# A recurrent-memory attention kernel with a gated feed-forward: Wo pieces multiplied in pairs, the late half of Wo moved behind two Wq pieces, a Wk eviction moved ahead, and the turning of x spread over the first step

## The chip, the cores and the metric

The kernel runs on one core of one Trainium2 chip. The metric is the time of one execution on the device in microseconds (us), as a median over runs; lower is better. The core's engines are TensorE (in the profile PE for matmuls and PEld for weight loads), VectorE (DVE), ScalarE (ACT), GpSimd (POOL) and SyncE (SP). SP, ACT and POOL issue DMAs; each has its own DMA queue. Each engine runs its own instructions strictly in the order in which the program lists them, and waits on semaphores for the others.

## The reference

Two branches over the same x of 2048 rows by 1024 (bfloat16) are mixed by a gate per row. Branch A is a transformer with a recurrent memory; branch B is a feed-forward.

```python
def _A_ref(x, mem0, Wq, Wk, Wv, Wo, seg_len):      # 32 heads of 128, M = 8, seg_len = 32
    ...
    for s in range(n_seg):                          # 64 segments
        xs = x[:, s * seg_len:(s + 1) * seg_len, :].copy()
        h = jnp.concatenate([mem, xs], axis=1)      # 8 + 32 = 40 rows
        q = jnp.einsum('btd,dhe->bhte', h, Wq)
        k = jnp.einsum('btd,dhe->bhte', h, Wk)
        v = jnp.einsum('btd,dhe->bhte', h, Wv)
        scores = jnp.einsum('bhqe,bhke->bhqk', q, k) * scale
        scores = jnp.where(mask[None, None], scores, -1000000000.0)
        p = _softmax(scores, axis=-1)
        o = jnp.einsum('bhqk,bhke->bhqe', p, v)
        o = jnp.einsum('bhte,hed->btd', o, Wo)
        mem = o[:, :M, :].copy()
        outs.append(o[:, M:, :])
    return jnp.concatenate(outs, axis=1)

def _B_ref(x, w_gate, w_up, w_down):
    return _gelu(x @ w_gate) * (x @ w_up) @ w_down

g = _sigmoid((x * gate_w).sum(-1, keepdims=True))
return g * a + (1 - g) * b
```

Each segment needs the memory rows that the segment before it produced, so the 64 segments form a chain.

## The kernel before

**Stages.** First the 16 tiles of x (128 rows each) are turned so that the model dimension lies on the partitions (`do_x`, L440). Then 64 steps run, one per segment. At the end the outputs of the rows that feed no memory are projected (L902 to L919), and the feed-forward follows (L951 on).

**Rows of a step.** The 40 rows of a segment are split. The 8 memory rows and 24 rows of x, 32 together, go through the step (`hT`). The remaining 8 rows of x are gathered from four segments at a time into a group of 32 rows (`hR`). Their projections are called fills: `fill` (L740) multiplies, `fill_evac` (L764) evicts, `fill_put` (L775) turns and writes to DRAM (`qk_scr`, `v_scr`). A step does one fill or two (`FILL`, L791; two in the steps after segments 0 and 1 of each four); `load_qk` (L476) and `load_v` (L481) fetch a segment's part back with POOL DMAs, `load_r` (L472) fetches the next group's rows. Where no second fill is to be done, `warm` (L754) multiplies for nothing.

**Weights.** Wq, Wk, Wv and Wo are each cut into 16 pieces of 512 KB: two halves of 16 heads (index u) by eight pieces i. All 64 do not fit into SBUF. Some places are held by a fixed piece; 14 are shared by the pieces (m, 0, i) and (m, 1, i) (`PAIRS`, L297: two each of Wk and Wq, four of Wv, six of Wo). A step works on one half first (r = 0) and on the other after it (r = 1), and the next step starts with the half that is there. So a shared place is loaded once per step, as soon as the piece of r = 0 has been multiplied (`spent`, L389); that is 14 loads of 512 KB per step, issued by SP. The copies of the shared Wo pieces in `wo_scr` are written in steps 1 to 12 (`keep`, L364) and read from then on.

**Order.** `HEAD` and `BODY` (L309, L310) list blocks of four pieces; `walk` (L315) makes of them the order of all pieces on TensorE:

```python
HEAD = [("k", 0, 0), ("o", 1, 1), ("q", 0, 0), ("v", 0, 0), ("k", 0, 1), ("q", 0, 1), ("v", 0, 1)]
BODY = [(m, r, h) for m, r in (("k", 1), ("q", 1), ("o", 0), ("v", 1)) for h in range(2)] + [("o", 1, 0)]
```

The block `("o", 1, 1)`, the late half of the second Wo half, belongs to the step before and runs after the first four Wk pieces of the new step. `seq` (L304) gives the order of the eight pieces of a half. `plan` (L807) hangs all other work on places of this walk: `on("q", 1, 2, f)` runs f just before piece 2 of Wq, r = 1. The place in the walk fixes an operation's place in the order of its engine, not only on TensorE: an operation of ACT, POOL or SP stands behind all operations of that engine that were hung on earlier places.

**One projection piece** (`proj`, L688): for q, k and v four matmuls of 512 columns (L699), one for each group of 32 partitions of the PSUM bank. A Wo piece (L711) is eight matmuls of 256 columns, into the half b = i // 4 of the columns of bank `XO`, with the heads j = i % 4.

**Attention of a half.** `evac` (L601) copies the projection from PSUM to a staging tile with ACT; `trans` turns it (four transposes, L611) and copies it with DVE (L597) into `kT` or `qT`. `put_rest` (POOL, L787) adds the eight rest columns to `kT`. `scores` (L624) multiplies (L627, L633) and runs the softmax down to `tAB`, the turned probabilities (L639 to L652). `attend` (L654) multiplies with `vA` (L661, L666), which ACT evicted from the Wv bank, and `take` copies the result to `oT`. `rest_o` (POOL) keeps the rest rows in `oRc`, from where SP writes them to DRAM (L872).

**Shared memory.** Staging tiles have no place of their own (L289): `stage["k"]` lies on `kT`, and so does `pAB`; `stage["q"]` lies on `qT`, and so does `tAB`; `stage["o"]` lies on `oT`, and so does `vA`. `oRc` (512 bytes per partition) and `a_bf` (512 bytes) follow each other. A writer waits until all readers of what lies there are done; for a DMA that reads, until it has landed.

**Memory chain.** When a half of the columns of Wo is complete, `fold` (L719) adds the two halves of the partitions with two DVE operations (L722, L723) into `a_bf`. `next_mem` (L726) turns the memory rows (two transposes, L732) and copies them (L735) into the next step's `hT`: half 0 before the first Wk piece, half 1 before piece 4. Piece i of Wk, Wq and Wv reads only chunk i of `hT`. `a_bf` is written to DRAM (`a_scr`) by a POOL DMA (L889).

**First step.** Before step 0, all 16 calls of `do_x` run: eight transposes into a PSUM bank, three copies (ACT and DVE), DMAs of the turned tile to DRAM (ACT's queue), the gate's product on POOL (L463, into one buffer `gp`) and its sum on DVE (L465). Eight buffers `px` hold x; a load of tile T + 8 waits for the product of tile T. The work buffers of this stage lie on the places of Wo. Then step 0 does seven fills itself (`fill0`, L802).

## Time and profile before

| | |
|---|---|
| median of 3 runs | 2394.21 us (2392.74 to 2399.93) |
| the profiled execution's own time | 2389.05 us |
| its span, first to last instruction | 2387.2 us |
| mean granted TensorE clock | 0.973 |
| busy share of the span: PE / PEld / DVE / ACT / POOL | 89% / 47% / 44% / 22% / 18% |
| DMA | 639.69 MB, mean 268 GB/s |
| scores of the first half in steps 0, 1 and 63 start at | 100.0, 142.4 and 1721.4 us |
| first feed-forward matmul starts at | 1799.2 us |

So the 64 steps take most of the span, about 25 us each after the first ones; the feed-forward takes the last 588 us. How to read the lines below: "busy" is the time in which an engine worked on the group; "idle before" is the time that the engine stood still just ahead of it, with what ended the wait. In the timeline each row is a start, a duration, the engine, the line of the kernel, the operation and what it writes and reads; x32 means that 32 like instructions were merged into one row. The chain of waits is the sequence of work that ended last, each link released by the one before. A matmul of a stream is shown with its whole latency, so of a row of n matmuls the pace is to be read and not the single duration.

### The profile page before, as it was taken

To read this page: it belongs to the slowest core of one execution; us is meant where nothing else is said; L and a number is where in the kernel's file an instruction comes from. 1 tells how busy PE (TensorE), PEld (TensorE's weight loads), DVE (VectorE), ACT (ScalarE), POOL (GpSimd) and SP (SyncE) were. 2 spreads that over 40 slices of the span, in tenths; PEclk is the share of its full clock that TensorE was granted. 3 is DMA by queue.
4 is the path that set the end of the run, shared out by engine and by line. 5 is a ranking of instruction groups with operands and counts; after the bars stand their busy time and mean duration, and the time that the engine had idled before them with its cause. 6 is when DMAs were issued, how large, how long until landed. Compare 5 with 4: busy or idle time off the path is not lost.

```text
span 2387.2 us, 78943 instructions
## 1 busy us (share of the span) xinstructions
PE 2135.7 (89%) x35875; PEld 1119.7 (47%) x35900; DVE 1050.7 (44%) x2438; ACT 515.9 (22%) x985; POOL 431.0 (18%) x821
## 2 busy tenths in 40 slices
PE   2588888898898999898998999988889999999999
PEld 1244444454454545444544555554454444444444
DVE  3244444444444444444444444454414436264363
ACT  1121212222222222222222222221203213032130
POOL 5222222222222222222222222221100000000000
PEclk6699999999999999999999999999999999999999
DMA  9889989998998989899898999998976160622530
GB/s 359 331 292 301 325 305 325 347 319 310 321 314 309 328 305 327 309 316 327 299 315 307 324 333 331 317 327 315 332 247 212 63 219 18 234 66 89 180 103 18
DMA packets 261469, 639.69 MB, mean 268 GB/s; under 512 B 28264, under 2 KB 102760, under 8 KB 261136
## 3 DMA queue, kind: packets, MB, share of 16 engines
q1 hardware_dynamic: 237312, 597.66, 71.6%
q0 software_dynamic: 13888, 26.31, 3.7%
q10 hardware_dynamic: 9936, 10.69, 1.3%
q8 instruction: 282, 4.62, 0.8%
q14 instruction: 51, 0.42, 0.1%
HBM read 596.85 MB, written 37.68 MB: 266 GB/s over the span
## 4 chain that ended last, share of the span: by engine, by line
PE 65%; DVE 14%; DMA 9%; issue 6%; ACT 5%; POOL 1%; ACTq 0%; POOLq 0%; SPq 0%
PE pb L699 16%; PE pb L960 14%; PE pb L711 9%; PE pb L1014 5%; PE pb L611 5%; PE pb L748 4%; DMA sl<-in_A_Wo_dram 3%; DVE tAB L652 3%; PE pb L911 2%; ACT kS L594 2%; PE pb L995 2%; PE pb L633 2%; DMA sl<-wo_scr 2%; PE pb L758 2%; DVE pb L640 2%
## 5 line engine op out<-in xcount | busy, mean ns | idle before, releaser
L699 PE MATMUL pb<-sl,hT 128*32 128x512 bf16 x12288 | 766.1, 382 | 7.7 <-issue 6.8
L699 PEld LDWEIGHTS pb<-sl,hT 128*32 128x32 bf16 x12288 | 350.3, 97 | 260.7 <-issue 16.6
L711 PE MATMUL pb<-sl,oT 128*32 128x256 bf16 x8192 | 307.3, 277 | 49.1 <-issue 29.7
L711 PEld LDWEIGHTS pb<-sl,oT 128*32 128x32 bf16 x8192 | 196.3, 97 | 121.1 <-issue 40.4
L748 PE MATMUL pb<-sl,hR 128*32 128x512 bf16 x3072 | 233.1, 397 | 15.2 <-issue 14.0
L960 PE MATMUL pb<-xT,wg 128*128 128x512 bf16 x896 | 211.7, 379 | 0.7
L960 PE MATMUL pb<-xT,wu 128*128 128x512 bf16 x896 | 211.6, 379 | 0.0
L594 ACT ACTIVATE kS<-pb 128x512 bf16<-128x512 f32 x190 | 113.4, 597 | 453.9 <-PE pb L699 359.8
L682 POOL COPY oRc<-oT 128x128 bf16<-128x128 bf16 x128 | 96.6, 754 | 345.2 <-DVE oT L597 342.7
L722 DVE COPY part<-pb 64x256 f32<-64x256 f32 x128 | 54.0, 422 | 229.0 <-PE pb L711 225.6
L597 DVE CAST oT<-pb 128x160 bf16<-128x160 f32 x382 | 105.6, 318 | 110.4 <-PE pb L666 110.4
L641 ACT ACTIVATE E<-pb 128x320 bf16<-128x320 f32 x128 | 55.9, 437 | 439.6 <-DVE pb L640 439.6
L1014 PE MATMUL pb<-wd,GT 128*128 128x512 bf16 x657 | 145.1, 379 | 2.7 <-DMA wd<-in_B_w_down_dram 1.9
L960 PEld LDWEIGHTS pb<-xT,wg 128*128 128x128 bf16 x896 | 87.2, 98 | 108.0 <-DVE GT L976 3.7
L597 DVE COPY kT<-pb 128x512 bf16<-128x512 bf16 x128 | 54.3, 424 | 188.4 <-PE pb L611 180.7
L960 PEld LDWEIGHTS pb<-xT,wu 128*128 128x128 bf16 x896 | 87.6, 98 | 105.7
L968 ACT ACTIVATE s<-pb 128x512 f32<-128x512 f32 x112 | 66.8, 596 | 312.3 <-PE pb L960 312.3
L969 DVE SCALAR_TENSOR_TENSOR tp<-s,pb 128x512 f32<-128x512 f32 x112 | 77.0, 687 | 124.7 <-ACT s L968 124.5
L639 DVE TENSOR_REDUCE st<-pb 128x8 f32<-128x320 f32 x128 | 63.0, 492 | 140.6 <-PE pb L633 140.6
L787 POOL COPY kT<-qkr 128x128 bf16<-128x128 bf16 x128 | 37.6, 294 | 460.0 <-DVE kT L597 368.8
L748 PEld LDWEIGHTS pb<-sl,hR 128*32 128x32 bf16 x3072 | 86.7, 99 | 70.9 <-issue 31.5
L973 DVE SCALAR_TENSOR_TENSOR tp<-tp,pb 128x512 f32<-128x512 f32 x112 | 77.0, 687 | 78.7 <-ACT tp L972 78.7
(84 smaller groups left out, 2096.7 us busy)
## 6 DMA issues: line engine op xcount, KB each, us to landing
sl<-wo_scr SPq DMA_DIRECT2D x342, 512.0 KB, 7.0
sl<-in_A_Wv_dram SPq DMA_DIRECT2D x268, 512.0 KB, 10.4
sl<-in_A_Wk_dram SPq DMA_DIRECT2D x142, 512.0 KB, 5.5
sl<-in_A_Wq_dram SPq DMA_DIRECT2D x142, 512.0 KB, 7.5
wd<-in_B_w_down_dram SPq DMA_DIRECT2D x42, 1024.0 KB, 5.6
sl<-in_A_Wo_dram SPq DMA_DIRECT2D x52, 512.0 KB, 7.7
wdF<-in_B_w_down_dram SPq DMA_DIRECT2D x7, 1024.0 KB, 7.8
wo_scr<-sl SPq DMA_DIRECT2D x12, 512.0 KB, 11.5
```

Of the source, the lines that this page charges most:

```text
L594: op("act", lambda e: e.activation(o, i, ACTF.Copy), rd=rd, wr=wr)
L597: op("dve", lambda e: e.tensor_copy(o, i), rd=rd, wr=wr)
L611: ins = e.transpose(PBV[TT][:, j * 128:(j + 1) * 128], st[:, j * 128:(j + 1) * 128], ident[:, :])
L652: op("dve", lambda e: e.transpose(tAB[:, :], pAB[:, 0:512]), rd=[pAB.r()], wr=[tAB.r()], after=[fin])
L682: op("pool", lambda e: e.tensor_copy(oRc[:, :, 16 * u:16 * u + 16].rearrange("p c x -> p x c"), oT[:, :, :, 32:40].rearrange("p g j c -> p ...
L699: ins = e.matmul(PB[bk][32 * g:32 * g + 32, :], lhsT=h[:, i, :], rhs=w[:, g * 512:(g + 1) * 512], start=(n == 0), stop=(n == 7))
L711: ins = e.matmul(PB[XO][32 * g:32 * g + 32, 256 * b:256 * b + 256], lhsT=oT[:, j, x, 0:32], rhs=w[:, c:c + 256], start=(r == 0 and n == 0 ...
L748: ins = e.matmul(PB[b][32 * g:32 * g + 32, :], lhsT=h[:, k[2], :], rhs=w[:, g * 512:(g + 1) * 512], start=(n == 0), stop=(n == 7))
L960: ins = e.matmul(PB[bk][:, 0:FB], lhsT=w[:, kc, cc:cc + 128], rhs=xT[:, :, :, kc, :].rearrange("p t i c -> p (t i) c"), start=(kc == 0), s ...
L969: op("dve", lambda e, hg=hg, t=t: e.scalar_tensor_tensor(out=t[:, :], in0=s1[:, :], scalar=1.0, in1=hg, op0=ALU.add, op1=ALU.mult), rd=[BK ...
L973: op("dve", lambda e, hu=hu, t=t: e.scalar_tensor_tensor(out=t[:, :], in0=t[:, :], scalar=1.0, in1=hu, op0=ALU.add, op1=ALU.mult), rd=[BK( ...
L1014: ins = e.matmul(PB[bank[2 * k + hf]][:, :], lhsT=GT[:, j, tb * 128:(tb + 1) * 128], rhs=w[:, jj, hf * 512:(hf + 1) * 512], start=(j == 0) ...
```

## The change

Four things are changed in the steps, and the start.

1. For r = 0, Wo pieces i and i + 4 (the same heads, the two halves of the columns) are multiplied together: eight matmuls of 512 columns in place of sixteen of 256. The places of Wo become one tensor `wall`, so that one operand can reach into two of them; the order is 0, 4, 1, 5, 2, 6, 3, 7, and both places are given back after the pair.
2. The late half of Wo (r = 1, pieces 4 to 7) runs after the first two Wq pieces of the next step. Its `fold`, the second fill's eviction and `load_v` move with it, from the place ahead of Wq piece 0 to that ahead of piece 2; `fill_put` goes from Wv piece 0 to 2 and `next_mem` of half 1 from Wv piece 1 to 3.
3. In steps 1 to 63 the second Wk half is evicted at Wq piece 1 (r = 1) and not at the start of Wo, into a new staging tile that lies on `oRc` and `a_bf`. The eviction into `vA` moves from Wq piece 2 to 3. The DMA that writes `a_bf` to `a_scr` moves from ("q", 1, 0) to ("k", 0, 4).
4. Four tiles of x are turned ahead of step 0 and the other twelve in it, in banks `XO` and `SS`; the gate and the loads follow them, and the fills of r = 1 in step 0 are hung on different Wq pieces.

```diff
-        stage = {n: al(n + "S", [128, 512], at=t.off) for n, t in (("k", kT), ("q", qT), ("o", oT))}
+        assert a_bf.off == oRc.off + 512
+        stage = {n: al(n + "S", [128, 512], at=t.off) for n, t in (("k", kT), ("q", qT), ("o", oT), ("p", oRc))}
...
+            if (m, r) == ("o", 0):
+                return [i + x for i in range(4) for x in (0, 4)]
...
-        HEAD = [("k", 0, 0), ("o", 1, 1), ("q", 0, 0), ("v", 0, 0), ("k", 0, 1), ("q", 0, 1), ("v", 0, 1)]
-        BODY = [(m, r, h) for m, r in (("k", 1), ("q", 1), ("o", 0), ("v", 1)) for h in range(2)] + [("o", 1, 0)]
+        HEAD = [("k", 0, 0, 4), ("q", 0, 0, 2), ("o", 1, 4, 8), ("q", 0, 2, 4), ("v", 0, 0, 4), ("k", 0, 4, 8), ("q", 0, 4, 8), ("v", 0, 4, 8)]
+        BODY = [(m, r, 0, 8) for m, r in (("k", 1), ("q", 1), ("o", 0), ("v", 1))] + [("o", 1, 0, 4)]
...
-        slots = [al(f"sl{n}", [128, 2048]) for n in range(len(hosts))]
+        nkqv = sum(h[0][0] != "o" for h in hosts)
+        slots = [al(f"sl{n}", [128, 2048]) for n in range(nkqv)]
+        wall = al("wall", [128, len(hosts) - nkqv, 2048])
+        slots += [_V(wall, n) for n in range(len(hosts) - nkqv)]
...
-            b = 6 + T % 2
+            b = (XO, SS)[T % 2]
...
-        for T in range(NT):
+        do_x(0)
+        load_h(0, "pool")
...
+        for T in range(1, min(NT, 4)):
             do_x(T)
...
+            elif r == 0:
+                j = i % 4
+                w4 = 4 * LQ
+                if n % 2 == 0:
+                    wa, wb = slots[home[k]], slots[home[k[0], k[1], i + 4]]
+                    na, nb = wa.n, wb.n
+
+                    def f(e):
+                        for hp in range(2):
+                            for g in range(4):
+                                x = 2 * hp + g // 2
+                                c = 512 * x + 256 * (g % 2)
+                                ins = e.matmul(PB[XO][32 * g:32 * g + 32, :], lhsT=oT[:, j, x, 0:32],
+                                               rhs=wall[:, na:nb + 1:nb - na, c:c + 256], start=(n == 0 and hp == 0),
+                                               stop=False, skip_group_check=True)
+                        return ins
+                    op("pe", f, rd=[oT.r(j * w4, (j + 1) * w4), wa.r(), wb.r()], wr=[BK(XO)])
+                if n % 2:
+                    spent((*k[:2], i - 4))
+                    spent(k)
+                return
...
             if s == 0:
+                on("k", 0, 0, lambda: some_x(4, 6))
                 on("k", 0, 0, lambda: fill0("k", 0, B0, "k"))
                 if NG > 1:
                     on("k", 0, 0, lambda: fill0("k", 0, B1, "o", 1, hR1))
-                on("k", 0, 0, lambda: [first(("o", u, i)) for u in range(2) for i in range(8)])
+                on("q", 0, 0, lambda: some_x(6, 8))
+                on("q", 0, 0, lambda: [load_x(NPX + n) for n in range(4, 8)])
+                on("q", 0, 0, lambda: (firsts("k", 1), firsts("q", 1)))
                 on("q", 0, 0, lambda: fill0("q", 0, B1, "q"))
+                on("v", 0, 0, lambda: some_x(8, 12))
                 on("v", 0, 0, lambda: fill0("v", 0, B2, "o"))
+                on("k", 0, 4, lambda: some_x(12, 16))
...
+                on("k", 0, 4, gate)
+                on("k", 0, 5, lambda: (firsts("v", 1), firsts("o", 0), firsts("o", 1)))
...
-            on(*(("k", 1, 1) if s == 0 else ("q", 1, 2)), lambda: evac(bank_of["v", 0], vA, "act"))
+            on(*(("k", 1, 1) if s == 0 else ("q", 1, 3)), lambda: evac(bank_of["v", 0], vA, "act"))
...
-            on("o", 0, 0, lambda: evac(bank_of["k", 1], stage["k"], "act"))
+            on(*(("q", 1, 1) if s else ("o", 0, 0)), lambda: evac(bank_of["k", 1], stage["p" if s else "k"], "act"))
             if s > 0:
                 on("o", 0, 0, lambda: attend(ua, ((0, "dve"), (1, "dve"))))
-            on("o", 0, 0, lambda: trans(kT, "k"))
+            on("o", 0, 0, lambda: trans(kT, "p" if s else "k"))
...
             if two:
-                on("q", 0, 0, lambda: fill_evac(*fl[1], B0, "o"), **nx)
-                on("v", 0, 0, lambda: fill_put(*fl[1], "o"), **nx)
-            on("q", 0, 0, lambda: fold(s, 1), **nx)
-            on("q", 0, 0, lambda: load_v(s + 1), **nx)
-            on("v", 0, 1, lambda: next_mem(s, 1), **nx)
-            on("q", 1, 0, lambda: op("pool", lambda e: e.dma_start(a_scr[s].rearrange("g r c -> (g r) c"), a_bf[:, :]), rd=[a_bf.r()],
+                on("q", 0, 2, lambda: fill_evac(*fl[1], B0, "o"), **nx)
+                on("v", 0, 2, lambda: fill_put(*fl[1], "o"), **nx)
+            on("q", 0, 2, lambda: fold(s, 1), **nx)
+            on("q", 0, 2, lambda: load_v(s + 1), **nx)
+            on("v", 0, 3, lambda: next_mem(s, 1), **nx)
+            on("k", 0, 4, lambda: op("pool", lambda e: e.dma_start(a_scr[s].rearrange("g r c -> (g r) c"), a_bf[:, :]), rd=[a_bf.r()],
                                      wr=[("D", "a", s)], lane="st"), **nx)
```

`_V` is a view of one place of `wall` with the same attributes as a tile of its own; `firsts(m, r)` issues the first load of the eight pieces of a half; `some_x(lo, hi)` calls `do_x` for those tiles; `gate` holds the three operations (L512 to L515) that turn the row sums into the gate.

66 lines of the change are left out of this document (36 added, 30 removed).

## Prediction

> **What bounds the kernel now.** I read the chain of waits first. By engine it says:
>
> ```profile
> PE 65%; DVE 14%; DMA 9%; issue 6%; ACT 5%; POOL 1%; ACTq 0%; POOLq 0%; SPq 0%
> ```
>
> TensorE sets two thirds; a third is work on which TensorE waits. The steps have to be opened one by one. I take step 35 and read the timeline by engine, from its first scores (L627 at 1022.29) to the second. TensorE:
>
> ```profile
> 1022.29 0.31 PE L627 MATMUL pb<-mS,ident 128*128 128x320 bf16 x1
> ...
> 1026.71 0.50 PE L661 MATMUL pb<-tAB,vA 32*128 32x40 bf16 x16
> 1027.04 0.20 PE L666 MATMUL pb<-tAB,vB 32*128 32x64 bf16 x4
> 1027.36 0.40 PE L611 MATMUL pb<-ident,kS 128*128 128x128 bf16 x4
> 1027.69 0.63 PE L711 MATMUL pb<-sl,oT 128*32 128x256 bf16 x16
> 1028.37 0.38 PE L611 MATMUL pb<-ident,qS 128*128 128x128 bf16 x4
> 1028.68 1.06 PE L711 MATMUL pb<-sl,oT 128*32 128x256 bf16 x32
> 1029.67 0.31 PE L627 MATMUL pb<-mS,ident 128*128 128x320 bf16 x1
> ```
>
> ACT and DVE in the same stretch:
>
> ```profile
> 1024.41 0.59 ACT L594 ACTIVATE vA<-pb 128x512 bf16<-128x512 f32 x1
> 1026.71 0.60 ACT L594 ACTIVATE kS<-pb 128x512 bf16<-128x512 f32 x1 [1.70 <-PE pb L699]
> 1027.30 0.60 ACT L594 ACTIVATE qS<-pb 128x512 bf16<-128x512 f32 x1
> ```
>
> ```profile
> 1027.30 0.56 DVE L597 CAST oT<-pb 128x160 bf16<-128x160 f32 x2 [0.69 <-PE pb L666]
> 1027.79 0.42 DVE L597 COPY kT<-pb 128x512 bf16<-128x512 bf16 x1
> 1028.14 0.55 DVE L597 CAST oT<-pb 128x160 bf16<-128x160 f32 x2
> 1028.79 0.42 DVE L597 COPY qT<-pb 128x512 bf16<-128x512 bf16 x1
> ```
>
> The attention of the first half starts at 1026.71, and the second scores at 1029.67, so 2.96 us later. In between TensorE turns K only after ACT has evicted it (1026.71 to 1027.31), and the eviction had waited for the softmax, since its staging tile lies on `pAB`. The vA eviction, done at 1025.00, is 1.7 us ahead of its use.
>
> **Part 1, paired pieces and an early Wk eviction.** First the pace of both kinds of matmul, from the chain of waits:
>
> ```profile
> 1039.37 0.86 PE pb L699 x16
> 1040.24 0.87 PE pb L711 x32
> ```
>
> 512 columns take 53.8 ns, 256 take 27.2: two merged matmuls cost what one wide one costs, so the merging gains nothing where matmuls stream at this pace. In the first Wo half they don't: there the 32 end 0.99 us after their start (1028.68 to 1029.67). The rest comes from the order. With K evicted beforehand, counted from the start A of the attention: its matmuls leave TensorE free at A+0.31; K is turned until A+0.71; the first oT copy ends at A+0.87 (1027.30 + 0.28), so pair 0 runs from A+0.93 to A+1.36 (8 x 53.8 ns); Q is turned until A+1.74, its eviction being done at A+1.19; pairs 1 and 2 end at A+2.60. On DVE the copies end about A+2.55. The scores start at A+2.62 and not A+2.96: **0.34 us less a step, 63 steps, -21 us**. Bounds: DVE, which has the same four copies, allows no more; if nothing but the eviction helped it would be 0.1 us, -6. The order 0, 4, 1, 5 lets piece 1 be fetched third and not second. It is used only after the eight Wv pieces (32 matmuls, 1.7 us), the second softmax and three more pieces, and I cost this at nothing; without that cover a load of 512 KB more ahead of it is 2.0 us at the mean 268 GB/s.
>
> **Part 2, what the early eviction waits for.** The new staging tile lies on `oRc` and `a_bf`, so the eviction must wait until the DMA that writes `a_bf` to DRAM has landed. In ACT's order vA stands behind it, and the attention waits for vA. POOL's timeline in step 35:
>
> ```profile
> 1017.95 0.55 POOL L482 DMA_DIRECT2D vB<-v_scr  x1 [3.61 <-DVE a_bf L723]
> 1018.49 0.56 POOL L473 DMA_DIRECT2D hR<-xr_scr  x1
> ...
> 1023.21 0.55 POOL L889 DMA_DIRECT2D a_scr<-a_bf  x1
> ```
>
> The DMA is moved from 1023.21 to right behind the vB load, where the hR load stands in this step. The late Wo half comes 8 matmuls later (8 x 53.8 ns = 0.43 us), so it is issued at 1018.49 + 0.43 = 1018.92. When it lands, the DMA issues of 300 to 1500 us bound (the last number is the median to landing):
>
> ```profile
> vB<-v_scr POOLq DMA_DIRECT2D x48, 64.0 KB, 6.7
> ...
> a_scr<-a_bf POOLq DMA_DIRECT2D x47, 64.0 KB, 5.8
> hR<-xr_scr POOLq DMA_DIRECT2D x12, 64.0 KB, 7.3
> ```
>
> By its own row (5.8, at its old place) it lands at 1024.7. Then come two evictions of 0.60 and 0.05 to the matmul: attention possible at 1026.0, and nothing is lost against 1026.71. By the hR row (the same size, the same place in the queue) it lands at 1026.2, the attention starts at 1027.5 and 0.8 us is lost. I take 0.7: the place behind the vB load counts for more than the direction. **63 x 0.7 = +44 us**, bounds 0 and, by a late vA below, 2.0 us (126). That a late vA stops TensorE is seen in step 33, where another DMA held it:
>
> ```profile
> 976.98 0.60 ACT L594 ACTIVATE vA<-pb 128x512 bf16<-128x512 f32 x1 [3.26 <-DMA qk_scr<-oS]
> 977.63 0.27 PE L661 MATMUL pb<-tAB,vA 32*128 32x40 bf16 x16 [2.03 <-ACT vA L594]
> ```
>
> The Trainium skill, page "DMA: Bandwidth & Descriptors", section "Anatomy of one DMA — SWDGE (gpsimd) path", gives about 2.0 us plus bytes over 436 GB/s per DMA. For 64 KB that would be, as an estimate from that page, 2.2 us, the DMA would be back 5 us before it is needed, and the sum would be 44 us lower. The trace disagrees: all three rows above are 2.6 to 3.3 times as long, with the other queue full of 512 KB loads.
>
> **Part 3, the late Wo half behind two Wq pieces.** The matmuls are the same, and their loads have 0.43 us more. What that can bring is bounded by the page's row of the Wo matmuls:
>
> ```profile
> L711 PE MATMUL pb<-sl,oT 128*32 128x256 bf16 x8192 | 307.3, 277 | 49.1 <-issue 29.7
> ```
>
> Of the 49.1 us idle ahead of them 29.7 have no releaser; 19.4 remain for all Wo matmuls and steps, so -19 at most; I take 0, since a load that is late by more than 0.43 us stays late. SP issues the two Wq loads about 1 us earlier (the 32 Wo matmuls, 0.87, no longer stand before them). The vB load on POOL goes 0.43 us later and, by its 6.7, lands at 1025.1, still ahead of the attention. What is lost is cover: after `next_mem` of half 1, three Wv pieces ran before Wk piece 4 needed its result, now one.
>
> ```profile
> 1017.74 0.23 PE L732 MATMUL pb<-ident,a_bf 64*128 64x64 bf16 x2
> ```
>
> ```profile
> 1018.00 0.17 DVE L735 COPY hT<-pb 128x32 bf16<-128x32 bf16 x1 [0.34 <-PE pb L732]
> ```
>
> The copy ends at 1018.17; with 0.05 for the semaphore and 0.1 for the weights (the first oT copy to the first Wo matmul above takes as long) Wk could start at 1018.33. One Wv piece (0.22) covers from 1017.97 to 1018.19. **0.15 us x 63 = +9 us**, bounds 0 and 0.25 (+16). The `fold` keeps its distance of five pieces; `fill_put` keeps its place one piece ahead.
>
> **Part 4, fewer instructions.** 32 matmuls and 32 weight loads a step are gone. TensorE has gaps with no releaser; its instructions come by DMA on a queue of their own (packets, MB, share of the engines' span):
>
> ```profile
> q8 instruction: 282, 4.62, 0.8%
> ```
>
> ```profile
> 1031.99 0.39 PE L748 MATMUL pb<-sl,hR 128*32 128x512 bf16 x1 [0.59 <-issue]
> ```
>
> The gaps follow the stretches of short matmuls, of which the first Wo half is one. "issue" is 6% of the chain, 143 us over the span; I take 0.1 us a step off, **-6 us**, bounds 0 and 0.25 (-16). The skill's page "Runtime: NRT & Kernel Launch", section "Instruction fetch mechanics", calls the crossing of a 16 KiB block mostly hidden. By it this term is 0 and the sum 6 us higher; the gap of 0.59 above speaks for the trace.
>
> **Part 5, the start.** POOL before and in step 0:
>
> ```profile
> 69.52 2.12 POOL L463 TENSOR_TENSOR gp<-px,gwb 128x1024 f32<-128x1024 bf16 x1 [1.93 <-DVE dl L465]
> 75.05 0.82 POOL L783 DMA_DIRECT2D qk_scr<-kS  x1 [3.42 <-DVE kS L780]
> 80.98 0.76 POOL L783 DMA_DIRECT2D qk_scr<-oS  x1 [5.11 <-DMA qk_scr<-kS]
> 87.64 0.75 POOL L783 DMA_DIRECT2D qk_scr<-qS  x1 [5.90 <-DMA qk_scr<-oS]
> 88.39 2.20 POOL L769 DMA_DIRECT2D v_scr<-oS  x4
> 94.21 0.56 POOL L478 DMA_DIRECT2D qkr<-qk_scr  x1 [3.62 <-DMA qk_scr<-qS]
> ```
>
> The first attention in step 0 follows at:
>
> ```profile
> 105.14 0.32 PE L661 MATMUL pb<-tAB,vA 32*128 32x40 bf16 x16 [4.32 <-DMA vB<-v_scr]
> ```
>
> The last product of x ends at 71.6, and only then come three writes of fills, one after another as they share a lane, before the loads that the first attention needs. In the change the fills of Wk and Wq run between the tiles, so their writes have landed long before the last product. They cost POOL their issue (3 x 0.8), the four v writes (2.2) and one wait of 5.1; the products end at 71.6 + 9.7 = 81, and the qkr load is issued there and not at 94.2: **-13 us**. Bounds: -21 if POOL lost nothing (94.2 less 73), 0 if the loads of Wo, whose places hold x until the last tile, decide step 0.
>
> **Sum.** -21 + 44 + 9 - 6 - 13 = +13 us on the profiled execution's own 2389.05 (its span is 2387.2). That execution lies 5.2 below the median of 2394.21; against the median the change gives **2407 us**, slower by 0.5%.
>
> **Rivals.**
> - *The write of a_bf is back in time* (place: ACT's eviction at Wq piece 1; it decides where the DMA lands before about 1025.4 in step 35, 6.5 us after its issue). For it: the a_scr row of 5.8, and the page's rule above, whose result this is; Wq loads that start earlier leave less in the queues. Against: the vB and hR rows. Then Part 2 is 0: 2407 - 44 = **2363 us, faster**.
> - *Half of it*: landing after 7.0 us, loss 0.45 us a step, +28: 2391, **no change**.
> - *The steps with two fills lose more*: there the write of the fill (oS, 128 KB) goes ahead of a_scr on POOL's queue, and it was this write that held vA in step 33. With 1.2 us on the average step, +76: 2439.
> - *The start gains nothing*, since step 0 ends with the Wo loads: 2407 + 13 = 2420.
>
> **How the numbers follow.** Forecast 0.38, with its own range of 2402 to 2424; in time 0.30; half 0.14; more at two fills 0.09; no gain at the start 0.09. 0.3% is 7 us, about what three runs can tell from no change. Faster 0.30, same 0.14, slower 0.38 + 0.09 + 0.09 = 0.56. The range of 2362 to 2438 leaves out half of the first rival and half of the fourth case, 0.2.
>
> **What would show it.** Part 2: waits of ACT on the DMA that writes a_scr, and of L661 on vA, together some 44 us; without them the first rival holds. Part 1: 2.6 us from the attention to the second scores in nearly every step. Part 3: waits of the Wk weight loads on the hT copy. Part 5: the first attention matmul near 91 us and not 105. The prediction is wrong if the a_scr write lands within 6.5 us in most steps, or if the second scores don't move closer to the attention.

## The result, and the profile after

The changed kernel takes **2376.6 us** (median of 4 runs, 2371.4 to 2381.0) against 2396.4 for the kernel before in the same session. The quotient of these two medians is 0.992; the measured ratio, with its 95% interval, is 0.9935 (0.9909 to 0.9962). By that ratio it is faster by 0.65%, where 0.5% slower was forecast. The profiled execution took 2371.4 us, its span is 2369.6, which is 17.6 less than before.

The changed kernel's page, its instruction queue (packets, MB, share) and the chain of waits by engine and by line:

```profile
q8 instruction: 266, 4.36, 0.7%
...
PE 48%; DMA 29%; DVE 8%; issue 7%; ACT 5%; POOL 3%; ACTq 0%; SPq 0%; POOLq 0%
DMA a_scr<-a_bf 16%; PE pb L1009 14%; DMA wall<-wo_scr 6%; PE pb L719 6%; PE pb L1063 6%; PE pb L735 5%; PE pb L752 3%; PE pb L789 3%; DMA wall<-in_A_Wo_dram 2%; PE pb L960 2%; PE pb L1044 2%; PE pb L631 2%; PE pb L799 2%; ACT pS L614 1%; DMA xr_scr<-xr 1%
```

TensorE held 65% of the chain before and DMA 9%. Now DMA holds 29%. Two different DMAs stand behind this. The first, 16% of the chain, was foreseen: the write of `a_bf`, for which the early eviction waits. In the waits by engine (who waits, for what: us in all, times, longest):

```profile
ACT pS L614 <- DMA a_scr<-a_bf: 95.4, 61, 3.6
```

and in step 33 on TensorE, ACT and POOL, one after the other:

```profile
961.05 0.31 PE L647 MATMUL pb<-mS,ident 128*128 128x320 bf16 x1
...
966.03 0.27 PE L681 MATMUL pb<-tAB,vA 32*128 32x40 bf16 x16 [0.87 <-ACT vA L614]
966.14 0.20 PE L686 MATMUL pb<-tAB,vB 32*128 32x64 bf16 x4
966.27 0.40 PE L631 MATMUL pb<-ident,pS 128*128 128x128 bf16 x4
966.79 0.61 PE L735 MATMUL pb<-wall,oT 128*32 128x512 bf16 x8
967.45 0.38 PE L631 MATMUL pb<-ident,qS 128*128 128x128 bf16 x4
967.76 1.05 PE L735 MATMUL pb<-wall,oT 128*32 128x512 bf16 x16
968.74 0.31 PE L647 MATMUL pb<-mS,ident 128*128 128x320 bf16 x1
```

```profile
964.89 0.60 ACT L614 ACTIVATE pS<-pb 128x512 bf16<-128x512 f32 x1 [1.61 <-DMA a_scr<-a_bf]
965.38 0.59 ACT L614 ACTIVATE vA<-pb 128x512 bf16<-128x512 f32 x1
```

```profile
957.81 0.55 POOL L938 DMA_DIRECT2D a_scr<-a_bf  x1
```

The write is issued at 957.81 and ACT goes on at 964.89, 7.1 us later. The attention follows 4.98 us after the first scores, and the second scores 2.71 us after the attention. That is the picture that Parts 1 and 2 drew, and yet the time fell. The second DMA in the chain is Wo's loads (`wall`, 6% and 2%). TensorE's groups between 150 and 1700 us (busy, mean ns | idle before, and what ended it; "issue" is idle time for which the profile shows no releaser) show both it and the gain. Before:

```profile
L711 PE MATMUL pb<-sl,oT 128*32 128x256 bf16 x7760 | 291.3, 277 | 46.4 <-issue 29.2 <-DMA sl<-in_A_Wo_dram 11.6 <-DMA sl<-wo_scr 2.2
L748 PE MATMUL pb<-sl,hR 128*32 128x512 bf16 x2784 | 209.6, 389 | 14.6 <-issue 14.0
...
L661 PE MATMUL pb<-tAB,vA 32*128 32x40 bf16 x1936 | 35.3, 177 | 40.6 <-issue 20.9 <-DVE tAB L652 15.1 <-ACT vA L594 2.7
```

After:

```profile
L789 PE MATMUL pb<-sl,hR 128*32 128x512 bf16 x2752 | 198.4, 385 | 8.6 <-issue 8.3
L752 PE MATMUL pb<-wall,oT 128*32 128x256 bf16 x3920 | 147.3, 276 | 35.5 <-DMA wall<-wo_scr 15.7 <-DMA wall<-in_A_Wo_dram 11.0 <-issue 6.3
L735 PE MATMUL pb<-wall,oT 128*32 128x512 bf16 x1952 | 144.1, 392 | 7.4 <-issue 0.2
...
L681 PE MATMUL pb<-tAB,vA 32*128 32x40 bf16 x1952 | 34.5, 178 | 70.9 <-ACT vA L614 42.7 <-DVE tAB L672 23.4 <-issue 4.1
```

Idle time without a releaser ahead of the Wo matmuls fell from 29.2 to 0.2 + 6.3 us, ahead of the attention from 20.9 to 4.1, ahead of the fills from 14.0 to 8.3. Two waits took the place of a good part of it: Wo's loads went from 13.8 to 26.7, vA from 2.7 to 42.7.

The mean step, from TensorE's rows of steps 2 to 62, in us (fold and `next_mem` of half 0, then of half 1, lie between the second attention and the next scores):

| stretch | before | after | forecast |
|---|---|---|---|
| first scores to first attention | 4.48 | 4.98 | +0.7 (Part 2) |
| first attention to second scores | 3.02 | 2.81 | -0.34 (Part 1) |
| second scores to second attention | 5.13 | 4.62 | -0.1 (Part 4) |
| second attention to `next_mem` of half 0 | 3.74 | 3.78 | |
| `next_mem` of half 0 to that of half 1 (two Wq pieces, 0.43, moved in) | 4.49 | 4.83 | |
| `next_mem` of half 1 to first scores (the same moved out) | 4.56 | 4.25 | +0.15 (Part 3) |
| step | 25.41 | 25.26 | +0.41 |

Outside these steps: the first scores come at 87.8 and not at 100.0, steps 0 and 1 together take 7.4 us longer, and what follows the first scores of step 63 is 3.4 shorter. Together -12.2 + 7.4 - 9.4 - 3.4 = -17.6. The last 3.4 should not be put down to the change: that stretch takes 665.6 to 667.5 us in the runs e1 to e8 below, 665.8 in the kernel before, and 662.4 in this execution alone.

### The profile page after: what moved, and what is told of

It reads as the page before. It is cut to its first block, busy times and chain, and to the rows that moved or that the text cites. A ratio compares the mean times of both kernels' runs of the same rounds, so it can differ in the third digit from the quotient of the medians.

```text
span 2369.6 us, 74769 instructions
## 1 busy us (share of the span) xinstructions
PE 2130.4 (90%) x33827; PEld 1054.9 (45%) x33852; DVE 1044.7 (44%) x2438; ACT 519.1 (22%) x985; POOL 432.9 (18%) x821
## 4 chain that ended last, share of the span: by engine, by line
PE 48%; DMA 29%; DVE 8%; issue 7%; ACT 5%; POOL 3%; ACTq 0%; SPq 0%; POOLq 0%
DMA a_scr<-a_bf 16%; PE pb L1009 14%; DMA wall<-wo_scr 6%; PE pb L719 6%; PE pb L1063 6%; PE pb L735 5%; PE pb L752 3%; PE pb L789 3%; DMA wall<-in_A_Wo_dram 2%; PE pb L960 2%; PE pb L1044 2%; PE pb L631 2%; PE pb L799 2%; ACT pS L614 1%; DMA xr_scr<-xr 1%
## 5 line engine op out<-in xcount | busy, mean ns | idle before, releaser
L719 PEld LDWEIGHTS pb<-sl,hT 128*32 128x32 bf16 x12288 | 342.4, 97 | 273.7 <-DVE hT L776 21.7
L789 PE MATMUL pb<-sl,hR 128*32 128x512 bf16 x3072 | 224.0, 393 | 9.2 <-issue 8.3
L752 PE MATMUL pb<-wall,oT 128*32 128x256 bf16 x4048 | 152.1, 276 | 38.0 <-DMA wall<-wo_scr 16.5
L735 PE MATMUL pb<-wall,oT 128*32 128x512 bf16 x2048 | 153.1, 396 | 7.6 <-issue 0.2
L614 ACT ACTIVATE kS<-pb 128x512 bf16<-128x512 f32 x127 | 75.8, 597 | 367.9 <-PE pb L719 349.2
L752 PEld LDWEIGHTS pb<-wall,oT 128*32 128x32 bf16 x4048 | 97.7, 97 | 93.8 <-issue 36.8
L789 PEld LDWEIGHTS pb<-sl,hR 128*32 128x32 bf16 x3072 | 84.7, 99 | 68.6 <-issue 20.9
```

Source lines behind the costliest of these rows:

```text
L614: op("act", lambda e: e.activation(o, i, ACTF.Copy), rd=rd, wr=wr)
L719: ins = e.matmul(PB[bk][32 * g:32 * g + 32, :], lhsT=h[:, i, :], rhs=w[:, g * 512:(g + 1) * 512], start=(n == 0), stop=(n == 7))
L735: ins = e.matmul(PB[XO][32 * g:32 * g + 32, :], lhsT=oT[:, j, x, 0:32], rhs=wall[:, na:nb + 1:nb - na, c:c + 256], start=(n == 0 and hp == 0),
L752: ins = e.matmul(PB[XO][32 * g:32 * g + 32, 256 * b:256 * b + 256], lhsT=oT[:, j, x, 0:32], rhs=w[:, c:c + 256], start=False, stop=(n % 4 ...
L789: ins = e.matmul(PB[b][32 * g:32 * g + 32, :], lhsT=h[:, k[2], :], rhs=w[:, g * 512:(g + 1) * 512], start=(n == 0), stop=(n == 7))
```

## The experiments

All times are medians; every run has its ratio to the kernel before, measured on the same chip in the same session. There were several sessions, on different chips, and the kernel before took 2387 to 2396 us in them. So the difference of two medians from different sessions can be off by several us; where that matters the difference by the ratios stands beside it, and the text says where the intervals overlap. The edits are shown shortened. The theories, A to F, are named in the expectations. The stretches are those of the table. "Gaps" are TensorE's idle times without a releaser between 150 and 1700 us, per step: 1413 ns before, 605 after. The sum takes in some shorter ones than the rows of the groups do, so it is larger, by up to about a fifth.

**1. Is it the number of instructions?** The merge was undone in the changed kernel, done alone in the kernel before, and done with as many instructions put back elsewhere.

```
e1_unmerged       changed kernel, per pair:
-  matmul(PB[XO][32g:32g+32, :],  rhs=wall[:, na:nb+1:nb-na, c:c+256])
+  for b in range(2): matmul(PB[XO][32g:32g+32, 256b:256b+256], rhs=wh[:, c:c+256])
e4_before_merge   kernel before + seq("o", 0) = 0, 4, 1, 5, 2, 6, 3, 7 + merged matmuls
e11_split_wv      e4_before_merge, second Wv half:
-  matmul(..., rhs=w[:, 512g:512g+512])
+  for c in (0, 256): matmul(..., rhs=w[:, 512g+c:512g+c+256])
```

> The changed kernel with each merged 512-column matmul of the first Wo half put back as two of 256 columns, in the same order of pieces; everything else as changed. Against the changed kernel (2376.6 us, 25.26 us a step; second scores to second attention 4.62 us, in the kernel before 5.13). Theory A, TensorE's instruction gaps follow the number of its instructions: the 32 matmuls and 32 weight loads a step come back, the stretch from the second scores to the second attention goes back to 5.1 us, and the time rises by 63 x 0.5 = 31 us to about 2407. Theory B, the gaps shrank because TensorE now waits 0.5 us a step for vA ahead of the attention and its instructions come in meanwhile: the stretch stays near 4.6 us, and the time stays within 7 us of 2377.

> The kernel before with only the merged matmuls in the first Wo half, and the order of pieces that they need. By the prediction's Part 4: 6 us less than before, 16 at most. Theory A: second scores to second attention 5.13 down to 4.62, 63 x 0.5 = 31 us less, ratio 0.987. Theory B: that stretch stays near 5.1, and the time within 0.3% of before.

> The kernel before with the merge alone, and in the second Wv half each matmul of 512 columns split into two of 256: the 32 matmuls and 32 weight loads a step that the merge took away come back at another place, with the same work. Theory A (TensorE's gaps follow the number of its instructions, wherever they stand): gaps without a releaser back from 771 to about 1400 ns a step, packets of TensorE's instruction queue back from 266 to 282, time back by about what the merge gave, 10 us or more: 2389 and above. Rival A2 (only the first Wo half was dense): gaps stay near 800 ns, the time within 7 us of 2379.

| | us | ratio (95%) | gaps, ns a step | second scores to second attention | step |
|---|---|---|---|---|---|
| e1_unmerged | 2390.7 | 1.0011 (0.9963 to 1.0059) | 1130 | 4.97 | 25.64 |
| e4_before_merge | 2379.0 | 0.9958 (0.9923 to 0.9994) | 771 | 4.56 | 25.19 |
| e11_split_wv | 2418.6 | 1.0111 (1.0074 to 1.0149) | 1744 | 4.89 | 25.76 |

Theory A holds for the gaps. The merge alone takes 0.64 us of gaps a step away; 64 instructions a step that do the same arithmetic at another place bring them back, and more (1744), and the instruction queue is back at 282 packets in that run. The groups of the kernel before with the merge alone:

```profile
L747 PE MATMUL pb<-wall,oT 128*32 128x256 bf16 x3936 | 154.1, 277 | 52.1 <-DMA wall<-wo_scr 25.4 <-DMA wall<-in_A_Wo_dram 18.3 <-issue 5.5
L730 PE MATMUL pb<-wall,oT 128*32 128x512 bf16 x1968 | 144.9, 389 | 2.6 <-issue 1.8
```

and of the one with the second Wv half split:

```profile
L789 PE MATMUL pb<-sl,hR 128*32 128x512 bf16 x2784 | 213.8, 394 | 24.1 <-issue 24.1
L752 PE MATMUL pb<-wall,oT 128*32 128x256 bf16 x3840 | 149.6, 283 | 45.5 <-issue 27.6 <-DMA wall<-in_A_Wo_dram 9.9 <-DMA wall<-wo_scr 6.4
...
L715 PE MATMUL pb<-sl,hT 128*32 128x256 bf16 x3840 | 124.0, 273 | 13.0 <-issue 12.8
```

The gaps need not stand at the split matmuls themselves (12.8): they show up at the Wo matmuls and the fills behind them (27.6 and 24.1). But theory B has a part as well: e1 has all instructions of before and yet 0.28 us less of gaps, and it is e1 that waits for vA; its time lies between the two theories. And the size is missing: 0.64 us a step would be 40 us, and the merge alone gave 10. In its first row the loads of Wo hold TensorE for 43.7 us, against 13.8 before. The new order of the loads alone does not do that: e1 has it too, with the old instructions (and a wait for vA), and waits 14.5 us for them:

```profile
L752 PE MATMUL pb<-wall,oT 128*32 128x256 bf16 x3880 | 143.9, 276 | 26.1 <-issue 9.5 <-DMA wall<-wo_scr 7.3 <-DMA wall<-in_A_Wo_dram 7.2
```

What the gaps wait for can be read from the traces, which have the time of every packet of the instruction queue. Of TensorE's idle times of more than 0.4 us between 150 and 1700 us, those without a releaser end 1.2 to 1.7 us after such a packet has landed: 53 of 53 in the kernel before (61.6 us in all), 24 of 24 with the merge alone (22.7 us), 64 of 64 with the second Wv half split (77.6 us), and 32 of 33 in the changed kernel (28.1 us). Of moments taken at random about 8% do, and of the waits with a releaser 3 of 24, 8 of 46, 4 of 17 and 7 of 73. So the gaps that the merge removes, and that the split brings back, are tied to the arrival of instructions.

**2. Do the loads take it back?** The reload of Wo's piece 4 is left out, in the kernel before and in the kernel before with the merge; in a third run only the order of the loads is changed.

```
e9_merge_fewer, e10_before_fewer     in fetch(n):
+  if k[0] == "o" and k[2] == 4 and done[n]: return
e7_fetch_order    changed kernel, loads behind the merged pairs:
-  0, 4, 1, 5, 6, 7
+  0, 1, 4, 5, 6, 7
```

> The kernel before with the merge alone (2379.0 us, 25.19 us a step, waits of TensorE on Wo loads 715 ns a step against 182 before) and the reload of Wo's piece 4 left out: its place is loaded once and serves both halves of the heads, so 512 KB of the 14 x 512 KB a step are not moved and the output is not the reference's. Theory F, the merge made TensorE 0.6 us a step faster (its instruction gaps 1413 to 771 ns) and the loads of Wo, issued in one burst when the first Wo half frees its places, took 0.5 us of it back: the waits on Wo loads fall below 250 ns, about 0.45 us a step, 28 us less: 2351. Rival, the loads only show a wait that another would replace: within 7 us of 2379.

> The kernel before with the same reload of Wo's piece 4 left out (the output is not the reference's). Theory F: before, instruction gaps and not loads set TensorE's pace, the waits on loads were 182 ns a step over all steps and 31 ns after step 10, so at most 0.15 us a step, 9 us less, ratio 0.996 to 1.000. Rival, the kernel before was bound by its loads as well: as much as in the run with the merge, some 28 us, ratio 0.988.

> The changed kernel with one thing moved: after the merged pairs of the first Wo half the loads are issued for piece 1 ahead of piece 4 (0, 1, 4, 5 and not 0, 4, 1, 5), so piece 4 goes one pair later. By the prediction, which cost the fetch of piece 1 in third place at nothing: within 7 us of 2377. Theory E: the waits of the second Wo half on its loads (162 ns a step ahead of its first four pieces, 17 before) come from that place; they go, 63 x 0.16 = 10 us less, 2367, more in steps 1 to 12.

With the merge 2379.0 became 2336.7 us (ratio 0.9779, 0.9742 to 0.9815), without it 2391.6 became 2368.8 (0.9906, 0.9870 to 0.9942). So loads bind both. For the kernel before the rival with 28 us comes nearer than theory F with 9: it gained 23. But the merge is worth 32 us when one load in 14 is gone (2368.8 - 2336.7) and 10 when it isn't. TensorE's Wo groups, without the load, with the merge and then without it:

```profile
L749 PE MATMUL pb<-wall,oT 128*32 128x256 bf16 x3984 | 147.1, 276 | 22.1 <-DMA wall<-in_A_Wo_dram 9.0 <-issue 7.0 <-DMA wall<-wo_scr 3.1
L732 PE MATMUL pb<-wall,oT 128*32 128x512 bf16 x2000 | 144.9, 385 | 1.3 <-issue 0.7
```

```profile
L713 PE MATMUL pb<-sl,oT 128*32 128x256 bf16 x7872 | 289.5, 276 | 31.5 <-issue 24.4 <-DMA sl<-in_A_Wo_dram 4.8 <-ACT oT L596 1.7
```

The same relief leaves 7.0 and 0.7 us without a releaser in the one and 24.4 in the other. Of all idle time ahead of the Wo matmuls it takes 31 us with the merge (52.1 and 2.6 became 22.1 and 1.3) and 15 without it (46.4 became 31.5). Theory F for the merge is shown; its sentence on the kernel before ("at most 0.15 us a step, 9 us less") was wrong by 14.

The order of the loads gives nothing: 2378.8 us, ratio 0.9931 (0.9905 to 0.9956). From the second attention to the fold of half 0 a step becomes 0.47 us shorter (2.75 to 2.28), and from `next_mem` of half 0 to the fold of half 1 it takes 0.60 more (3.55 to 4.15): piece 1 is in time, and the late half is late instead. The six loads are one burst, and which of them is late is all that their order decides.

**3. What does the wait for the write of a_bf cost?** ACT's order exchanged; the early eviction undone; the write issued by ACT's queue.

```
e2_va_first    - ("q", 1, 3): vA    ("q", 1, 1): pS      + ("q", 1, 1): vA    ("q", 1, 3): pS
e3_late_k      - ("q", 1, 1): evac(bank_of["k", 1], stage["p"])    + ("o", 0, 0): evac(bank_of["k", 1], stage["k"])
e8_a_scr_act   - op("pool", dma_start(a_scr[s] <- a_bf))    + op("act", dma_start(a_scr[s] <- a_bf))
```

> The changed kernel with the two evictions on ACT exchanged: vA at Wq piece 1, the second Wk half (which waits for the write of a_bf) at Wq piece 3. Nothing but the order on ACT changes. Theory A (gaps follow the number of instructions): the wait of the attention for vA, 0.70 us a step, goes; first scores to first attention 4.98 back to 4.48, the other stretches stay, 63 x 0.5 = 31 us less: about 2346. Theory B (the gaps shrank because of that wait): first scores to first attention 4.48, but second scores to second attention back from 4.62 toward 5.1, and the time stays within 7 us of 2377. A third outcome: the turn of K now waits for the Wk eviction instead, first attention to second scores rises from 2.81 to about 3.0, and 19 us are left of the gain: 2358.

> The changed kernel with the second Wk half evicted at the first Wo piece into the tile it had before, so that nothing waits for the write of a_bf; the rest as changed. By the prediction's Parts 1 and 2 undoing the early eviction gives 44 - 21 = 23 us back: about 2354. Theory A: first scores to first attention 4.98 back to 4.48, first attention to second scores 2.81 up to 3.0, second scores to second attention stays 4.62: 63 x (0.5 - 0.2) = 19 us less, about 2358. Theory B: the last stretch goes back to 5.1 as well, 63 x 0.2 = 13 us more, about 2389.

> The changed kernel with the write of a_bf issued by ACT, whose queue is empty in the steps, and not by POOL behind the vB load; same place in the program, the early eviction and ACT's order stay. If Part 2 is the place in POOL's queue, the write lands at least 0.7 us earlier against the first scores (3.6 now), vA is no longer late, first scores to first attention 4.98 back to 4.48. By the prediction's Part 2 that gives 44 us: 2333; by the stretch alone 31: 2346. Theory B (a wait of TensorE lets instructions and Wo loads catch up): 0.2 to 0.3 us a step come back as gaps and waits on Wo loads, 12 to 19 us are left: 2358 to 2365. If ACT's issue costs more than it gives: no change.

| | us | ratio (95%) | gaps, ns | first scores to attention | attention to second scores | step |
|---|---|---|---|---|---|---|
| changed kernel | 2376.6 | 0.9935 (0.9909 to 0.9962) | 605 | 4.98 | 2.81 | 25.26 |
| e2_va_first | 2368.0 | 0.9902 (0.9870 to 0.9934) | 776 | 4.52 | 3.01 | 25.14 |
| e3_late_k | 2366.7 | 0.9904 (0.9870 to 0.9937) | 838 | 4.64 | 3.05 | 25.13 |
| e8_a_scr_act | 2375.1 | 0.9938 (0.9910 to 0.9966) | 538 | 4.99 | 2.95 | 25.24 |

Undoing the early eviction gives 10 us (7 by the ratios, whose intervals overlap), where Parts 1 and 2 together had 23. Without the wait 0.46 us a step go at the attention, but the gaps grow by 0.17 to 0.23 and 0.2 come back before the second scores; the step keeps 0.12. The third run is a miss that teaches: on a queue that is empty in the steps the write takes longer. DMA issues of 300 to 1500 us of that run (KB each, median us to landing):

```profile
a_scr<-a_bf ACTq DMA_DIRECT2D x48, 64.0 KB, 8.1
vB<-v_scr POOLq DMA_DIRECT2D x48, 64.0 KB, 6.8
```

and of the changed kernel:

```profile
a_scr<-a_bf POOLq DMA_DIRECT2D x47, 64.0 KB, 7.0
```

ACT issues it 1.3 us earlier on the mean (4.64 against 3.35 us ahead of the first scores), and it lands 0.1 us earlier (3.58 against 3.68 us behind them). What it waits for is then not the vB load ahead of it on POOL's queue.

**4. The same with the loads relieved.** One reload is moved: Wo's piece 1 gets two places of its own, and Wv's piece 4 shares one. The 14 loads a step remain, but the burst behind the first Wo half has five. (The order of the pieces of Wo and Wv for r = 1 follows `PAIRS` and shifts with it.) It is made in three versions: vA first, ACT's order as changed, and the late eviction.

```
- PAIRS = {..., "v": (0, 1, 2, 3),    "o": (0, 1, 4, 5, 6, 7)}
+ PAIRS = {..., "v": (0, 1, 2, 3, 4), "o": (0, 4, 5, 6, 7)}
e12_pairs = e2_va_first + this    e13_after_pairs = changed kernel + this    e14_late_k_pairs = e3_late_k + this
```

> The version with vA evicted first (2368.0 us), with one reload moved: Wo's piece 1 gets two places of its own, and Wv's piece 4 shares one for both halves. As many loads a step, but five and not six in the burst behind the first Wo half. Theory F: TensorE's waits on Wo loads (476 ns a step) fall by half, 0.2 to 0.3 us a step, 12 to 19 us less: 2349 to 2356. If the load of Wv piece 4 comes too late in its place, waits on Wv loads show up instead: within 7 us of 2368.

> The changed kernel with only the reload moved from Wo piece 1 to Wv piece 4 (ACT's order as changed, so vA waits behind the second Wk eviction). Against the version with vA first and the same move (2345.1 us, 24.79 us a step). If Part 2's wait costs what its stretch shows once loads don't cover it (first scores to first attention 4.98 against 4.57): 63 x 0.4 = 25 us more, 2370. If the wait lets TensorE's instructions come in and shortens its later gaps (931 ns a step in that version), 10 to 15 us more: 2355 to 2360.

> The version with the second Wk half evicted late (2366.7 us) and the reload moved. By the prediction's Part 1 the early eviction is worth 0.34 us a step, so this is 21 us above the version with vA first and the reload moved: 2366. By the stretch from the first attention to the second scores in the traces (2.81 early, 3.05 late, 2.89 with vA first) 0.15 us a step, 10 us above: 2355. If the early eviction gains nothing that ACT's wait for the write does not take: within 7 us of 2345.

| | us | ratio (95%) | gaps, ns | wait for vA, ns a step | step |
|---|---|---|---|---|---|
| e12_pairs | 2345.1 | 0.9800 (0.9759 to 0.9840) | 931 | 98 | 24.79 |
| e13_after_pairs | 2361.8 | 0.9890 (0.9852 to 0.9929) | 501 | 856 | 24.96 |
| e14_late_k_pairs | 2344.1 | 0.9811 (0.9781 to 0.9842) | 735 | 83 | 24.62 |

Moving one reload gives 23 us with vA first (2368.0 to 2345.1), 15 in the changed kernel and 23 with the late eviction; by the ratios 24, 11 and 22, and for the 11 the intervals overlap. **e12 and e14 beat both kernels**, with intervals that lie below the changed kernel's; between the two of them the intervals overlap. e13 against e12 is the price of Part 2's wait with little else to hide it: 16.7 us by the medians of two sessions, or 0.27 us a step; in the two traces a step differs by 0.17 (24.96 and 24.79). TensorE waits 0.76 us a step longer for vA and has 0.43 fewer gaps. In the groups, e12 and then e13:

```profile
L681 PE MATMUL pb<-tAB,vA 32*128 32x40 bf16 x2000 | 36.1, 178 | 38.6 <-DVE tAB L672 17.9 <-issue 8.6 <-ACT vA L614 5.8
```

```profile
L681 PE MATMUL pb<-tAB,vA 32*128 32x40 bf16 x1984 | 34.9, 177 | 70.2 <-ACT vA L614 52.1 <-DVE tAB L672 14.4 <-issue 2.2
```

This is theory B in its right size: a wait is paid in part by gaps that would have come anyway. And e14 against e12 says that the early eviction, with ACT's order mended, gains nothing that these runs can tell.

**5. The late Wo half (Part 3).** In the changed kernel and in e12 the late half went back ahead of the four Wq pieces; in a last run neither it nor the early eviction is there.

```
- HEAD = k 0-3, q 0-1, late Wo, q 2-3, v 0-3, ...    fold, load_v at ("q", 0, 2)    next_mem(s, 1) at ("v", 0, 3)
+ HEAD = k 0-3, late Wo, q 0-3, v 0-3, ...           fold, load_v at ("q", 0, 0)    next_mem(s, 1) at ("v", 0, 1)
e6_head_old: changed kernel    e15_head_old_pairs: e12_pairs    e16_late_k_head_old_pairs: e14_late_k_pairs
```

> The changed kernel with the late Wo half back ahead of all four Wq pieces, and fold, the vB load and next_mem of half 1 at their old pieces. By the prediction's Part 3 (late Wo taken as 0, lost cover 9 us) undoing it gives 9 us back: about 2368. Theory D: TensorE, with fewer instruction gaps, now runs up against the loads of Wo (with the merge alone, in the old order, its waits on them were 715 ns a step, in the changed kernel 364), so the late half comes too early again: waits on Wo loads up by 0.2 to 0.35 us a step, cover back 0.12, 5 to 14 us more: 2382 to 2391.

> The version with vA first and the reload moved (2345.1 us), with the late Wo half back ahead of all four Wq pieces and fold, the vB load and next_mem of half 1 at their old pieces. By the prediction's Part 3 (lost cover 0.15 us a step, late Wo nothing): 9 us less, 2336. By the stretches of the run with the old place (half 1's next_mem to first scores 4.25 up to 4.56 for the two Wq pieces less 0.12 of cover; half 0's next_mem to fold of half 1 3.55 down to 3.23): within 7 us of 2345.

> Merge, new start and the reload moved alone: neither the early eviction nor the late Wo half of the change. By the prediction's sum for Parts 1 to 3 (-21 + 44 + 9) this is 32 us below the changed kernel with the reload moved. If Part 1 is a gain of 10 and Part 3 a loss of 8 us against the version with vA first, it is near 2347. It tells whether the two edits beside the merge and the start earn anything.

2382.2 us (ratio 0.9943, 0.9921 to 0.9964) against 2376.6; 2352.2 (0.9843, 0.9808 to 0.9878) against 2345.1; 2348.0 (0.9829, 0.9806 to 0.9852) against 2344.1. Three times the old place is 4 to 7 us worse (2 to 10 by the ratios), and each time the intervals overlap. Theory D's waits are there, but smaller: in steps 2 to 62 of e6 TensorE waits 0.50 us a step for Wo's loads, in the changed kernel 0.36. The move is at best a small gain and nowhere the loss of 9 that was forecast.

**6. The start (Part 5).** The changed kernel with the start of before.

```
- do_x(0..3), fills and their writes between some_x(4, 6), some_x(6, 8), some_x(8, 12), some_x(12, 16)
+ do_x(0..15), then fill0("k"), fill0("q"), fill0("v")
```

> The changed kernel with the start of before: all of x turned ahead of the first step, the fills and their writes behind it; from step 1 on as changed. By the prediction's Part 5 undoing it costs 13 us: about 2390. Theory C, from the traces: the first scores come 12 us later (100 and not 87.8), but steps 0 and 1, which were 1.9 and 5.5 us longer in the changed kernel, get that back, since Wo's loads, which hold them, are issued no later than before: about 5 us more, 2382.

2386.9 us, ratio 0.9968 (0.9943 to 0.9993): 10 us more than the changed kernel (8 by the ratios, whose intervals overlap), between the two theories. Steps 0 and 1 are 6.2 us shorter in it (72.5 against 78.8), as theory C has it. That part of the gain is given back is seen in the changed kernel's step 1:

```profile
147.46 0.40 PE L752 MATMUL pb<-wall,oT 128*32 128x256 bf16 x8 [1.25 <-DMA wall<-in_A_Wo_dram]
153.53 0.62 PE L752 MATMUL pb<-wall,oT 128*32 128x256 bf16 x8 [5.67 <-DMA wall<-in_A_Wo_dram]
```

but not all of it: the first scores of step 2 still come 6.7 us earlier than in e5 (166.55 and 173.28), and 4.8 earlier than in the kernel before (171.37).

## Why the prediction was wrong

**The step that failed is Part 4**: "I take 0.1 us a step off, -6 us, bounds 0 and 0.25 (-16)". The mechanism was named and the size missed. The gaps, of which this term takes off 0.1 us a step, fell by 0.81 (1413 to 605 ns), by 0.64 with the merge alone, and second scores to second attention became 0.51 us shorter. Of the difference of 0.56 us a step between forecast (+0.41) and trace (-0.15) this one term is 0.41. Its upper bound was too low by the prediction's own rows: Part 3 quotes 29.7 us without a releaser ahead of the Wo matmuls, 0.46 us a step, and puts only the other 19.4 to use. And that row isn't all, since gaps also went at the attention and the fills. Part 1's sentence that "the merging gains nothing where matmuls stream at this pace" is true of the pace and beside the point: the same columns in half the instructions don't run faster, they stall less.

In time the term is smaller than in that stretch, since Wo's loads took much of it back, and the other parts missed as well. The runs that undo one part in the changed kernel say, in us:

| | forecast | measured, by medians | by ratios | from |
|---|---|---|---|---|
| Parts 1 and 2 | +23 | +10 | +7 | e3_late_k |
| Part 3 | +9 | -6 | -2 | e6_head_old |
| Part 4 | -6 | -14 | -18 | e1_unmerged |
| Part 5 | -13 | -10 | -8 | e5_start_old |
| sum | +13 | -20 | -21 | |

The change itself gave -20 by the medians and -16 by the ratio. Only e1's interval does not overlap the changed kernel's, so the shares of the others are not firm. What Parts 2 to 4 have in common is the gaps: taken as nearly fixed, they leave a wait to be paid in full (Part 2) and the loads without effect (Part 3).

**Part 1** (-21): the direction is right, the size 0.21 us a step and not 0.34. The attention-to-scores stretch was 2.81 on the mean, not 2.62; in step 33 the first Wo pair starts 0.76 us behind the attention, where 0.93 was worked out, but the scores come at 2.71. With ACT's order mended, early and late eviction take the same time, so the gain is not shown in any total.

**Part 2** (+44): the mechanism and its place are right, down to the 7 us from issue to landing (the forecast leaned on a row of 7.3; the row is 7.0, and 50 of 61 took longer than 6.5), the 61 waits of ACT and vA behind it. The wait on vA grew by 0.66 us a step (2.7 to 42.7 us in the rows above, over 61 steps) and the stretch by 0.50. That is the rival "half of it" (landing after 7.0, loss 0.45) rather than the 0.7 taken. The step lost less still: with Part 1's gain taken off, 10 us in the run that undoes both, and 0.17 to 0.27 us a step with the loads relieved. The sum added the wait to gaps that it shortens. The reason given for the 0.7, "the place behind the vB load counts for more than the direction", fell: on an empty queue the write was no quicker.

**Part 3** (+9): the loss of cover is there, 0.12 us from `next_mem` to the scores once the 0.43 that moved is added back, as forecast 0.15. But the 0 taken for the late Wo half was wrong: TensorE, with fewer gaps, runs up against Wo's loads, and the 0.43 us that they gain is worth about as much as the cover, or a little more, as far as overlapping intervals tell. The argument that "a load that is late by more than 0.43 us stays late" says nothing of the time saved meanwhile.

**Part 5** (-13): right in its mechanism and at its place; the first attention came at 92.73 (near 91 forecast), the first scores 12.2 us earlier. What lasts is less, since step 1 waits 6.9 us for Wo's loads in the two lines above: 4.8 us at the first scores of step 2; undone it cost 8 to 10.

The rival "the write is back in time" had a chance of 0.30 and a time of 2363, and would have been right on the sign for a wrong reason: the write was late in nearly every step. No rival had the merge as a large gain with the loads of Wo as the new bound, and the range held the time only because that rival reached down to it.

## What to carry to other kernels

Before costing an edit that merges small instructions, add up the idle time without a releaser ahead of them and of what follows: that, and not the pace of the stream, is what fewer instructions can give. Then ask which transfer is in time only because of those gaps; here one burst of six loads took back most of the gain (the merge gave 10 us with it, 32 with one of its loads left out), and sharing it out differently gave another 22 to 24 us where vA did not wait behind the write of `a_bf`. Waits and gaps on one engine are not added: a wait of 0.76 us a step cost 0.17 to 0.27.

## What the runs showed of the hardware

TensorE's instructions come 16 KB at a time (4.62 MB in 282 packets), and 64 of them more or less in each of 64 steps are 16 packets. How the stalls follow was not expected: from 771 to 1744 ns a step with 64 instructions more in an unchanged stream of columns (merge alone against second Wv half split), and down to 501 where TensorE waits for something else. That the stalls are the fetching of instructions fits all of these runs, and the long ones end 1.2 to 1.7 us behind a landing packet of instructions (53 of 53 in the kernel before); no run changed the fetching by itself. The Trainium skill, page "Runtime: NRT & Kernel Launch", section "Instruction fetch mechanics", calls the crossing of a block mostly hidden; in these traces it is not hidden for about one packet in five: between 150 and 1700 us of the kernel before 53 stalls of more than 0.4 us come on 244 packets.

The 64 KB write of `a_bf` alone on its queue took 8.1 us, behind others on POOL's 7.0, and 5.8 at the old place of before, 4.3 us later in the step. The queue was not what it waited for. What the three have in common is the burst of 512 KB loads on SP's queue, with the 16 DMA engines 92% busy over the steps:

```profile
300.00:1500.00 1200.00, 1088.18 (x22860) 551.08 (x22852) 551.99 (x1482) 273.79 (x550) 291.28 (x580) 0.99 0.92 320
```

(the last three numbers are the granted clock, the DMA share and GB/s). That the engines, shared by all queues, set the latency is an inference from this; a run with the loads held off at that moment wasn't made.
